# One pool of eight PSUM banks for a fused attention and gated-unit kernel, with the scores of each head in a bank of their own

## The chip, the cores and the metric

The kernel runs on one core of a Trainium2 chip. The metric is the device time of one execution in microseconds (us); the time of a kernel is the median of its runs. Engines are named as the profile names them: PE is TensorE (PEld its weight loads), DVE is VectorE, ACT is ScalarE, POOL is GpSimd, SP is SyncE, which issues the DMAs.

## What is computed

Causal attention with a decay for 8 batches, 8 heads, 576 tokens and 64 features a head, then a gated linear unit with a causal convolution over 5 tokens on the 512 concatenated features (all in fp32 at the borders):

```python
scores = q @ k.T / 8                          # per batch and head, 576 x 576
cum    = cumsum(max(s, 0))
scores = where(causal, -1e9, scores + min(-(cum_i - cum_j), 0))
x      = softmax(scores) @ v                  # heads side by side: 576 x 512 per batch
gate   = sigmoid(sum_k conv_w[k] * x shifted by 4 - k tokens)
out    = (gate * (x @ w_val)) @ w_out
```

## The kernel before

The work is cut into 32 units. Unit n is batch b = n // 4 and head pair p = n % 4, with the head of the pair written hh = 0 or 1. Each unit goes through the same chain, and each link is one task with a name in the code:

- qk_T(b, p) transposes queries and keys of the pair on PE into a PSUM bank, qk_evac copies them out on ACT. tail_T and tail_evac do the same for the last 64 tokens.
- scores(n, step), step 0 to 2, on PE: the causal blocks of the 576 x 576 scores in three steps of 512 columns for each head. Two heads share the 128 rows of PE, so these matmuls use 64 rows each; the planner calls that mode "R" and everything else on PE mode "N". scores4(b, ...) does the last 64 tokens of all four pairs.
- exps(n, step) on ACT: the exponential of one step, from PSUM to the tile P. exp4 is the one for scores4.
- av(n, hh) on PE: 15 matmuls, attention times V', where V' (vprime, on POOL) is V with the decay weights and a column that gives the row sum.
- norm(n) on DVE: two reciprocals (L600) and two multiplications (L602) into xn.
- x_T(n) on PE transposes xn into a bank; x_evac(n) on DVE (L615) copies it to xT.
- tap(n, 0) to tap(n, 4): the five terms of the convolution into gp (L624 on ACT for tap 0 of odd units, else L626 and L628 on DVE). They read the bank of x_T, which is free only after tap 4. tanh(n) on ACT makes the gate.
- val(n, hf) on PE, two halves of the tokens: x @ w_val, for which all four x_evac of the batch must be done. glu(n, hf) on DVE (L659) multiplies with the gate.
- outp(b, i) on PE, out_evac on ACT, store on SP: the second product, five blocks of tokens a batch.

PSUM has eight banks here: four of a kind "m" for everything but scores, and two of a kind "s", each of which is two banks wide and holds one step of scores for both heads:

```python
plan = Plan(dict(m=4, s=2, P=3, gp=2, th=6, ot=3, qkf=3))
ps = slot[tok] = psum.tile([128, 2, 512], FP32, name=f"s{slot['s', tok]}")
nc.scalar.activation(out=slot["Pt", n][:, :, step * 512:(step + 1) * 512], in_=slot["s", n, step], func=AF.Exp, scale=0.125)
```

No loop sets the order of the instructions. Every task is given to a planner (class Plan) with its engine, an estimated duration, a due time (its place in units plus an offset of the table DUE), the tasks that it depends on and the buffers that it takes and gives back. Plan.run plays the tasks through once on the host, in each engine taking the ready task with the earliest due time, and the program is written out in that order. On the chip each engine works its own list strictly in order and waits by semaphore for what it needs. So the durations in the planner set the order, and the chip sets the times. On PE the planner has a rule of its own for going from mode N to mode R and back.

Loads go through SP in the planner's order: queries and keys of a batch (1 MB each, into three buffers "qkf", which POOL casts to bf16), the tails, V, and once the weights w_val (wv), w_out (wo) and conv_w (cw), the last transposed by conv_T on PE and copied to cwT on DVE (L478). Every tap reads cwT.

## Time and profile before

| | |
|---|---|
| time, median of 3 runs | 239.57 us (238.95 to 239.82) |
| time of the profiled execution | 239.43 us |
| its span, first to last instruction | 237.6 us |
| DVE busy | 193.1 us (81%) |
| PE busy | 190.1 us (80%) |
| ACT busy | 184.9 us (78%) |
| POOL busy | 73.5 us (31%) |
| first tap on DVE | 30.98 us |
| last glu on DVE ends | about 225.4 us |

The time lies 1.83 us above the span. Busy time counts an engine's instructions once where they overlap: on ACT and DVE the next instruction starts before the one ahead of it has ended, so the distance from start to start is shorter than the duration that a row gives. A wait in square brackets is time in which the engine stood idle just ahead of that instruction, with the instruction that ended the wait.

### The profile page before, as it was taken

The page shows a single profiled execution, that of the slowest core. Times are in us where ns is not written, and L with a number is a line of the kernel's source. Part 1 is how long each engine was busy: PE and PEld are TensorE (multiplying, and loading weights), DVE is VectorE, ACT ScalarE, POOL GpSimd, SP SyncE. Part 2 cuts the span into 40 slices and gives each one's busy share as a digit, 9 for nine tenths or more (in the row PEclk, how much of TensorE's full clock was granted, in tenths as well). Part 3 has the DMA queues.
Part 4 walks back from the last instruction along what each step waited for, and adds up shares of the span by engine and source line. Part 5 has one row for each costly group of instructions (what it writes and reads, how often), then busy time and mean ns, then how long its engine had stood idle before and what let it go on. Part 6 is the DMA issues. An engine that isn't in the chain of part 4 may idle for free. (4 is left out here: it accounts for less than half of the span.)

```text
span 237.6 us, 6221 instructions
## 1 busy us (share of the span) xinstructions
PE 190.1 (80%) x2561; PEld 124.4 (52%) x2561; DVE 193.1 (81%) x390; ACT 184.9 (78%) x241; POOL 73.5 (31%) x73
## 2 busy tenths in 40 slices
PE   0868746897898999769778797999899998878870
PEld 0546543565656756546546455656666655545420
DVE  4435599999999796998784996999999999999800
ACT  3588878986999999665987678997998998934340
POOL 8400434653953391004910158053035000000000
PEclk9999998899999999988999999999999999999997
DMA  5999789999989987995781402942681120123252
GB/s 153 266 277 375 179 192 320 287 193 243 353 197 263 280 230 229 265 185 179 226 176 29 132 3 87 192 81 88 157 158 44 47 91 22 47 88 110 107 189 75
DMA packets 69230, 40.49 MB, mean 170 GB/s; under 512 B 47109, under 2 KB 63493, under 8 KB 69194
## 3 DMA queue, kind: packets, MB, share of 16 engines
q1 hardware_dynamic: 69194, 40.01, 62.2%
q8 instruction: 22, 0.36, 0.6%
q14 instruction: 14, 0.11, 0.2%
HBM read 30.57 MB, written 9.44 MB: 168 GB/s over the span
## 5 line engine op out<-in xcount | busy, mean ns | idle before, releaser
L628 DVE SCALAR_TENSOR_TENSOR gp<-m,cwT,gp 128x572 f32<-128x572 bf16 (+3 forms) x128 | 103.7, 812 | 5.1 <-ACT gp L624 2.8
L583 ACT ACTIVATE P<-s 128x1024 bf16<-128x1024 f32 x96 | 94.8, 1039 | 11.9 <-PE s L580 8.4
L538 PE MATMUL s<-QKT 64*128 64x128 bf16 (+4 forms) x576 | 40.6, 247 | 10.0 <-ACT P L583 7.4
L500 POOL TENSOR_TENSOR Vp<-vst,w 128x650 bf16<-128x650 f32 x28 | 35.1, 1282 | 40.2 <-DMA vst<-in_v_dram 20.6
L653 PE MATMUL m<-xT,wv 128*128 128x288 bf16 x256 | 40.5, 293 | 7.7 <-DVE glu L659 5.5
L593 PE MATMUL m<-Vp,P 128*128 128x65 bf16 x960 | 39.3, 197 | 4.4 <-DVE gp L628 1.2
L665 PE MATMUL m<-wo,glu 128*128 128x512 bf16 x160 | 40.2, 380 | 2.2 <-DVE gp L628 1.0
L593 PEld LDWEIGHTS <-P 128*128 128x128 bf16 x960 | 35.0, 100 | 12.6 <-issue 3.6
L538 PEld LDWEIGHTS <-QKT 64*128 64x128 bf16 x576 | 20.6, 96 | 27.6 <-issue 18.9
L533 ACT COPY QKT<-m 128x1024 bf16<-128x1024 bf16 x32 | 32.2, 1031 | 3.5 <-PE m L529 3.4
L653 PEld LDWEIGHTS <-wv 128*128 128x128 bf16 x256 | 24.1, 99 | 20.6 <-issue 12.7
L670 ACT COPY ot<-m 128x512 f32<-128x512 f32 (+1 forms) x40 | 23.9, 598 | 14.0 <-PE m L665 11.7
L659 DVE SCALAR_TENSOR_TENSOR glu<-th,m 128x288 bf16<-128x288 f32 x64 | 27.8, 448 | 5.1 <-PE m L653 4.8
L602 DVE TENSOR_TENSOR xn<-m,recs 128x320 bf16<-128x320 f32 x64 | 28.1, 481 | 0.0
L633 ACT ACTIVATE th<-gp 128x576 f32<-128x576 f32 x32 | 22.4, 701 | 6.7 <-DVE gp L628 6.6
L665 PEld LDWEIGHTS <-glu 128*128 128x128 bf16 x160 | 14.2, 98 | 15.5 <-issue 3.6
L529 PE MATMUL m<-ident,qb 128*128 128x128 bf16 x128 | 13.1, 228 | 11.3 <-DVE chalf L432 6.1
L490 POOL CAST qb<-qkf 128x2048 bf16<-128x2048 f32 x7 | 13.2, 1891 | 25.1 <-DMA qkf<-in_q_dram 17.7
L600 DVE RECIPROCAL recs<-m 128x5 f32<-128x5 f32 x64 | 9.2, 176 | 11.0 <-PE m L593 11.0
L529 PEld LDWEIGHTS <-qb 128*128 128x128 bf16 x128 | 8.7, 101 | 16.6 <-issue 7.7
L611 PE MATMUL m<-ident,xn 128*128 128x128 bf16 x160 | 14.3, 220 | 3.6 <-DVE xn L602 2.7
L615 DVE COPY xT<-m 128x576 bf16<-128x576 bf16 x32 | 14.5, 452 | 2.8 <-PE m L611 2.6
(58 smaller groups left out, 151.1 us busy)
## 6 DMA issues: line engine op xcount, KB each, us to landing
out_dram<-ot SPq DMA_DIRECT2D x32, 256.0 KB, 2.1
qkf<-in_q_dram SPq DMA_DIRECT2D x7, 1024.0 KB, 8.6
qkf<-in_k_dram SPq DMA_DIRECT2D x7, 1024.0 KB, 8.8
vst<-in_v_dram SPq DMA_DIRECT2D x28, 256.0 KB, 5.2
vst<-in_v_dram SPq DMA_DIRECT2D x15, 128.0 KB, 4.1
first<-in_q_dram SPq DMA_DIRECT2D x4, 256.0 KB, 3.6
first<-in_k_dram SPq DMA_DIRECT2D x4, 256.0 KB, 3.7
tail<-in_q_dram SPq DMA_DIRECT2D x8, 128.0 KB, 7.7
```

The costliest lines, as they stand in the source:

```text
L500: eng.tensor_tensor(Vps[b % 2][:, :, h], vst[:, :, h], w[:, :, b * 8 + 2 * p:b * 8 + 2 * p + 2].unsqueeze(3).to_broadcast([128, NKB, 2, 65 ...
L533: nc.scalar.copy(QKTs[b % 2][:, :, p, 0:512].rearrange("d w (x j) -> d w x j", j=4), slot["qt", b, p].rearrange("d w (j x) -> d w x j", j=4))
L538: nc.tensor.matmul(ps[:, hh, c0:c0 + nq], QKTs[b % 2][r, 1, p, k0:k0 + 128], QKTs[b % 2][r, 0, p, q0:q0 + nq], **kw)
L583: nc.scalar.activation(out=slot["Pt", n][:, :, step * 512:(step + 1) * 512], in_=slot["s", n, step], func=AF.Exp, scale=0.125)
L593: nc.tensor.matmul(ps[:, qb * 65:qb * 65 + 65], lhsT, Vps[b % 2][:, kb, 2 * p + hh, :], start=(kb == 0), stop=(kb == qb))
L602: nc.vector.tensor_tensor(xns[b % 2][:, :, p * 128 + hh * 64:p * 128 + hh * 64 + 64], pvs[hh][:, :, 0:64], recs[:, n, hh].unsqueeze(2).to_ ...
L628: nc.vector.scalar_tensor_tensor(gp[:, sh:S], x[:, 0:S - sh], cwT[:, c, 4 - sh:5 - sh], gp[:, sh:S], ALU.mult, ALU.add)
L633: nc.scalar.activation(out=th, in_=slot["g", n], func=AF.Tanh, scale=0.5)
L653: nc.tensor.matmul(ps, wv[:, dc, c * 128:(c + 1) * 128], xTs[b % 2][:, dc, 4 + o:4 + o + 288], start=(dc == 0), stop=(dc == 3))
L659: nc.vector.scalar_tensor_tensor(glus[b % 2][:, c, o], slot["t", n][:, o], 1.0, slot["v", n, hf], ALU.add, ALU.mult)
L665: nc.tensor.matmul(ps, glus[b % 2][:, c, WIN[i]:WIN[i] + 128], wo[:, c, :], start=(c == 0), stop=(c == 3))
L670: nc.scalar.copy(ot[r, :], slot["o", b, i][r, :])
```

## The change

Four things change, and the arithmetic does not.

The pool: all eight banks are of one kind, and a step of scores takes two of them, one for each head. Each head's exponential is its own instruction of 512 columns and gives its bank back by itself; so 96 exponentials of 1024 columns become 192 of 512, and the 11 of exp4 become 22.

The planner's choice: of all tasks that are ready on an engine the one with the lowest due time goes first; on PE a task of the other mode has 0.28 (into R) or 13.36 (into N) added to its due time. The old rule on modes is gone.

The table DUE has new numbers, and some durations too (a tap 0.67 to 0.73, norm 1.1 to 1.02).

Some dependencies are put on an earlier task: qk_T and tail_T now wait in the plan for the old scores that qk_evac and tail_evac waited for, x_T for the old val, scores4 and av for what their readers waited for.

```diff
-DUE = dict(av=0.17, norm=-1.06, xt=0.72, xe=0.23, tap=1.91, dtap=0.12, ...
+DUE = dict(av=1.08, norm=-15.2, xt=1.96, xe=-1.95, tap=2.26, dtap=0.21, ...
+STAY = (0.28, 13.36)
...
-                for t in todo[e]:
-                    at = ready_at(t)
...
+                for t in ready[e]:
+                    at = can(t)
...
+                    key = t["key"] + (STAY[t["mode"] == "N"] if e == "PE" and t["mode"] != mode else 0)
+                    if pick is None or (key, t["n"]) < pick[:2]:
+                        pick = (key, t["n"], t)
...
-    plan = Plan(dict(m=4, s=2, P=3, gp=2, th=6, ot=3, qkf=3))
+    plan = Plan(dict(m=8, P=3, gp=2, th=6, ot=3, qkf=3))
...
-        nc.tensor.matmul(ps[:, hh, c0:c0 + nq], QKTs[b % 2][r, 1, p, k0:k0 + 128],
+        nc.tensor.matmul(ps[hh][:, c0:c0 + nq], QKTs[b % 2][r, 1, p, k0:k0 + 128],
...
-        ps = slot[tok] = psum.tile([128, 2, 512], FP32, name=f"s{slot['s', tok]}")
+        slot[tok] = [bank(tok + (hh,), [128, 512]) for hh in range(2)]
...
-    def exps(n, step):
-        nc.scalar.activation(out=slot["Pt", n][:, :, step * 512:(step + 1) * 512], in_=slot["s", n, step],
+    def exps(n, step, hh):
+        nc.scalar.activation(out=slot["Pt", n][:, hh, step * 512:(step + 1) * 512], in_=slot["s", n, step][hh],
...
-                take = [("s", ("s", n, i))] + ([("P", n)] if i == 0 else [])
+                take = [("m", ("s", n, i, hh)) for hh in range(2)] + ([("P", n)] if i == 0 else [])
...
-                es.append(add("ACT", 0.905, n + 0.3 * i, lambda n=n, i=i: exps(n, i), [t],
-                              give=[("s", ("s", n, i))]))
+                es += [add("ACT", 0.48, n + 0.3 * i + 0.01 * hh, lambda n=n, i=i, hh=hh: exps(n, i, hh), [t],
+                           give=[("m", ("s", n, i, hh))]) for hh in range(2)]
```

Since the planner's choice and numbers change, the order on every engine changes. Three places:

On DVE at the start, from the normalisation of unit 1 to the first tap (recs and xn are norm's, wv the cast of w_val, xT the x_evac). Before:

```order
L602 TENSOR_TENSOR xn_116<-m_402,recs 128x5x64
L455 TENSOR_SCALAR wv<-qkf_169 128x2048
L615 COPY xT_118<-m_440 128x576
L600 RECIPROCAL recs<-m_471 128x5
L600 RECIPROCAL recs<-m_487 128x5
```

After, with unit 2's normalisation now ahead of wv and unit 3's behind it, and then cwT and the taps:

```order
L585 TENSOR_TENSOR xn_116<-m_508,recs 128x5x64
L438 TENSOR_SCALAR wv<-qkf_175 128x2048
L583 RECIPROCAL recs<-m_548 128x5
L583 RECIPROCAL recs<-m_612 128x5
L585 TENSOR_TENSOR xn_116<-m_548,recs 128x5x64
L585 TENSOR_TENSOR xn_116<-m_612,recs 128x5x64
L461 COPY cwT<-m_629 128x20
L609 TENSOR_SCALAR gp_388<-m_387,cwT 128x576
```

The cast of w_val moved from behind unit 1 to between units 2 and 3. On SP the load of w_val moved too: from ahead of batch 1's queries, keys and tail to behind them, and that of conv_w stays behind it.

On PE at the same time, behind the last matmul of av(3, 0) (m_515 before, m_548 after). Before, av(3, 1) follows at once:

```order
L593 MATMUL m_515<-Vp_114,P_449 128x65
L593 LDWEIGHTS P_100
L593 MATMUL m_515<-Vp_114,P_100 128x65
L593 LDWEIGHTS P_449
L593 MATMUL m_533<-Vp_114,P_449 128x65
```

After, the transposes of batch 1 (four qk_T and a tail_T) follow, and av(3, 1) and conv_T come behind them:

```order
L576 MATMUL m_548<-Vp_114,P_458 128x65
L576 LDWEIGHTS P_100
L576 MATMUL m_548<-Vp_114,P_100 128x65
L512 LDWEIGHTS qb_105
L512 MATMUL m_566<-ident,qb_105 128x128
```

What moved here are 36 transposes, ahead of the second half of unit 3's attention, on which norm(3), cwT and every tap wait.

On DVE at x_evac of unit 11, the last of batch 2 (glu_120 with th_1439 or th_1593 is the first glu of that batch). Before:

```order
L615 COPY xT_118<-m_1647 128x576
L659 SCALAR_TENSOR_TENSOR glu_120<-th_1439,m_1683 128x288
L659 SCALAR_TENSOR_TENSOR glu_120<-th_1439,m_1691 128x288
L628 SCALAR_TENSOR_TENSOR gp_1648<-m_1647,cwT,gp_1648 128x572
L659 SCALAR_TENSOR_TENSOR glu_120<-th_1596,m_1698 128x288
```

After:

```order
L598 COPY xT_118<-m_1688 128x576
L611 SCALAR_TENSOR_TENSOR gp_1607<-m_1606,cwT,gp_1607 128x574
L611 SCALAR_TENSOR_TENSOR gp_1607<-m_1606,cwT,gp_1607 128x575
L642 SCALAR_TENSOR_TENSOR glu_120<-th_1593,m_1722 128x288
L642 SCALAR_TENSOR_TENSOR glu_120<-th_1593,m_1729 128x288
L642 SCALAR_TENSOR_TENSOR glu_120<-th_1658,m_1735 128x288
L611 SCALAR_TENSOR_TENSOR gp_1689<-m_1688,cwT,gp_1689 128x572
```

Two taps of unit 10 now stand between the copy and the glu, which needs val, which needs the copy.

## Rows read from the trace of the kernel before

**Rows 1.** The page, part 1: busy us, share of span, instructions.

```profile
PE 190.1 (80%) x2561; PEld 124.4 (52%) x2561; DVE 193.1 (81%) x390; ACT 184.9 (78%) x241; POOL 73.5 (31%) x73
```

**Rows 2.** Windows: length, PE, PEld, DVE, ACT, POOL busy, clock, DMA, GB/s.

```profile
31.00:61.00 30.00, 22.40 (x335) 15.63 (x331) 29.47 (x52) 25.50 (x32) 14.82 (x13) 0.94 0.96 255
61.00:151.00 90.00, 76.39 (x1081) 51.13 (x1077) 76.55 (x156) 75.81 (x98) 36.74 (x27) 0.98 0.69 184
151.00:226.00 75.00, 67.81 (x861) 42.63 (x861) 71.97 (x148) 59.73 (x81) 10.00 (x8) 1.00 0.36 95
226.00:237.60 11.60, 4.30 (x21) 1.67 (x19) 0.14 (x1) 3.35 (x6) 0.00 (x0) 0.88 0.38 124
```

**Rows 3.** Waits of DVE, 31 to 226 us: total us, times, longest.

```profile
DVE glu L659 <- PE m L653: 4.8, 6, 1.2
DVE recs L600 <- PE m L593: 3.5, 6, 1.0
DVE gp L628 <- ACT gp L624: 2.8, 5, 1.7
DVE xT L615 <- PE m L611: 2.6, 5, 0.8
```

**Rows 4.** Timeline of DVE: start, us, instruction, [idle before <-releaser].

```profile
92.72 0.45 DVE L659 SCALAR_TENSOR_TENSOR glu<-th,m 128x288 bf16<-128x288 f32 x1 [1.24 <-PE m L653]
...
119.07 1.67 DVE L628 SCALAR_TENSOR_TENSOR gp<-m,cwT,gp 128x572 f32<-128x572 bf16 x2 [1.72 <-ACT gp L624]
...
129.31 0.46 DVE L615 COPY xT<-m 128x576 bf16<-128x576 bf16 x1 [0.55 <-PE m L611]
```

**Rows 5.** Timeline of DVE, two taps of one unit, then a glu.

```profile
121.01 1.66 DVE L628 SCALAR_TENSOR_TENSOR gp<-m,cwT,gp 128x574 f32<-128x574 bf16 x2
122.59 0.45 DVE L659 SCALAR_TENSOR_TENSOR glu<-th,m 128x288 bf16<-128x288 f32 x1
```

**Rows 6.** Timeline of DVE at the start.

```profile
24.06 1.22 DVE L455 TENSOR_SCALAR wv<-qkf 128x2048 bf16<-128x2048 f32 x1
...
29.23 0.19 DVE L600 RECIPROCAL recs<-m 128x5 f32<-128x5 f32 x1 [0.99 <-PE m L593]
...
30.98 0.82 DVE L626 TENSOR_SCALAR gp<-m,cwT 128x576 f32<-128x576 bf16 x1
```

**Rows 7.** Timeline of POOL, the casts of batch 1's queries and keys.

```profile
25.50 1.89 POOL L490 CAST qb<-qkf 128x2048 bf16<-128x2048 f32 x1 [16.90 <-DMA qkf<-in_q_dram]
28.80 1.89 POOL L490 CAST kb<-qkf 128x2048 bf16<-128x2048 f32 x1 [1.41 <-DMA qkf<-in_k_dram]
```

**Rows 8.** Timeline of PE, the last av of unit 3.

```profile
28.68 0.97 PE L593 MATMUL m<-Vp,P 128*128 128x65 bf16 x26 [0.50 <-ACT P L583]
```

**Rows 9.** Groups by line: busy us, mean ns | idle before, releaser.

```profile
L583 ACT ACTIVATE P<-s 128x1024 bf16<-128x1024 f32 x96 | 94.8, 1039 | 11.9 <-PE s L580 8.4
L533 ACT COPY QKT<-m 128x1024 bf16<-128x1024 bf16 x32 | 32.2, 1031 | 3.5 <-PE m L529 3.4
```

**Rows 10.** Timeline of ACT, exponentials of 512 and 1024 columns in a run.

```profile
63.49 0.60 ACT L670 COPY ot<-m 128x512 f32<-128x512 f32 x1
63.95 0.64 ACT L558 ACTIVATE P<-s 128x512 bf16<-128x512 f32 x1
64.44 1.07 ACT L583 ACTIVATE P<-s 128x1024 bf16<-128x1024 f32 x1
65.34 0.64 ACT L521 COPY QKT<-m 128x512 bf16<-128x512 bf16 x1
```

**Rows 11.** Windows in which ACT is fullest; columns as in rows 2.

```profile
60.00:80.00 20.00, 18.03 (x269) 12.15 (x269) 18.64 (x41) 19.49 (x26) 10.41 (x7) 1.00 0.99 257
140.00:160.00 20.00, 17.38 (x238) 11.27 (x238) 17.61 (x36) 19.24 (x26) 10.45 (x9) 1.00 0.48 107
180.00:200.00 20.00, 19.60 (x283) 12.29 (x281) 19.19 (x40) 19.29 (x26) 1.17 (x1) 1.00 0.17 61
```

**Rows 12.** Waits of PE, 31 to 222 us: total us, times, longest.

```profile
PE s L538 <- ACT P L583: 5.5, 12, 1.3
```

More of the change, by code (lines that the diff above doesn't have):

```diff
@@ L220 @@
 NEG = -30000.0
[L224 to L226 removed]
+DUE = dict(av=1.08, norm=-15.2, xt=1.96, xe=-1.95, tap=2.26, dtap=0.21, tanh=3.88, cpe=-1.58, val=4.62,
+           dval=0.97, out=12.49, dout=0.2, oute=12.42, qt=-3.05, qe=4.97, tt=-2, te=-24.47, s4=0.17,
+           vp=-16.42, cast=4.1, lqk=-10.33, lv=-7.3)
+STAY = (0.28, 13.36)
 ON_PE = ()
@@ L252, in run, with can @@
     def run(self):
+        engs = ["SP", "POOL", "PE", "ACT", "DVE"]
         free = {k: [(0.0, i) for i in range(n)] for k, n in self.bufs.items()}
[L254 to L278 removed]
+        idle_at = dict.fromkeys(engs, 0.0)
+        ready = {e: [] for e in engs}
+        after = [[] for _ in self.tasks]
+        for t in self.tasks:
+            t["at"] = 0.0
+            names = {d["n"] for d in t["deps"]}
+            t["left"] = len(names)
+            for i in names:
+                after[i].append(t)
+            if not names:
+                ready[t["eng"]].append(t)
+        mode, dma_free, now = "N", 0.0, 0.0
+        self.order = []
+        def can(t):
+            at = t["at"]
+            for kind in {kind for kind, _ in t["take"]}:
+                c = sum(other == kind for other, _ in t["take"])
+                if len(free[kind]) < c:
+                    return None
+                at = max(at, sorted(free[kind])[c - 1][0])
+            return at
+        while len(self.order) < len(self.tasks):
+            started, later = False, []
             for e in engs:
                 if idle_at[e] > now + 1e-9:
[L281 removed]
+                    later.append(idle_at[e])
                     continue
                 pick = None
[L284 to L289 removed]
+                for t in ready[e]:
+                    at = can(t)
                     if at is None:
@@ L323, in run @@
                 for kind, tok in t["take"]:
-                    slot = min(free[kind])
-                    free[kind].remove(slot)
-                    self.slot[kind, tok] = slot[1]
+                    got = min(free[kind])
+                    free[kind].remove(got)
+                    self.slot[kind, tok] = got[1]
+                t["start"] = now
                 if e == "SP":
@@ L334, in run @@
                     free[kind].append((t["done"] + self.LAG, self.slot[kind, tok]))
-                todo[e].remove(t)
-                t["start"] = start
-                order.append(t)
-                left -= 1
+                ready[e].remove(t)
+                self.order.append(t)
+                later.append(idle_at[e])
                 started = True
-                nxt.append(idle_at[e])
-            if started:
-                continue
-            nxt = [x for x in nxt if x > now + 1e-9]
-            assert nxt, [(e, [(t["key"], t["emit"]) for t in todo[e][:3]]) for e in engs]
-            now = min(nxt)
-        self.order = order
-        return max(t["done"] for t in order)
+                for o in after[t["n"]]:
+                    o["at"] = max(o["at"], t["done"] + (self.LAG if o["eng"] != e else 0.0))
+                    o["left"] -= 1
+                    if o["left"] == 0:
+                        ready[o["eng"]].append(o)
+            if not started:
+                assert later
+                now = min(later)
+        return max(t["done"] for t in self.order)
 def main_path(ctx, tc, q, k, v, s, moe_w_val, moe_conv_w, moe_w_out, out, okcnt):
@@ L563, in scores @@
         b, p = divmod(n, 4)
-        ps = score_bank(("s", n, step))
+        ps = score_banks(("s", n, step))
         if step == 0:
@@ L752, in main_path @@
             on_pe = PE_CONV(b, p)
-            t = T["xt", n] = add("PE", 0.3, n + DUE["xt"], lambda n=n: x_T(n), ns,
-                                 take=[("m", ("x", n))] + ([] if on_pe else [("gp", n)]), mode="N")
+            t = T["xt", n] = add("PE", 0.3, n + DUE["xt"], lambda n=n: x_T(n),
+                                 ns + [T.get(("val", n0 - 8 + c, hf)) for c in range(4) for hf in range(2)],
+                                 take=[("m", ("x", n))] + ([] if on_pe else [("gp", n)]))
             T["xe", n] = add("DVE", 0.37, n + DUE["xe"], lambda n=n: x_evac(n),
```

114 lines of the change are left out of this document (33 added, 81 removed).

## The prediction

> **What bounds the kernel now.** I read the busy shares first. DVE, PE and ACT lie within 3% of each other, each near 80% [rows 1], so the totals name no bound. The windows do: from the first tap at about 31 us to the last glu at about 226 us DVE is busy 29.47 of 30, 76.55 of 90 and 71.97 of 75 us, together 178.0 of 195 [rows 2]. PE reaches 166.6 and ACT 161.0 in the same 195 us. So DVE sets the pace in the first and the last of the three windows, and in the middle one, where all three engines are busy some 85% of 90 us, they wait for each other in turn. Ahead of 31 us DVE has nothing to do but wait for the first units, and the last 11.6 us are the last output blocks and their stores, with DVE nearly idle [rows 2]; the order of that tail is almost the same in the changed kernel, so I leave it as it is.
>
> The span is therefore: the time of the first tap, plus DVE's work, plus DVE's waits, plus the tail. The waits are 4.8 + 3.5 + 2.8 + 2.6 = 13.7 us in 22 pieces [rows 3]; the 3.3 us that are missing to 17.0 are gaps too short for that view. DVE executes the same instructions after the change, so what can move is the first tap, the waits, and how tightly the taps follow each other.
>
> **The change, part by part.** The sum is made on the span of 237.6 us.
>
> *The waits of DVE: -6.7 us.* Most of them are round trips: DVE hands something to PE or ACT and then has too little other work until it comes back. Three kinds show in the rows. A glu straight behind the last x_evac of its batch stood 1.24 us, the time of val on PE; a tap 1 behind its own x_evac waited 1.72 us for tap 0 on ACT; an x_evac straight behind its norm waited 0.55 us for x_T [rows 4]. In the order of the instructions I counted the places where less than about 1 us of other DVE work stands in such a round trip (for the third kind, none or one short instruction), from unit 2 on. Before there are 12: 2, 7 and 3 of the three kinds. After there are 5: two glu (batches 3 and 5; the first is also a tap 1 place), two more tap 1 (units 19 and 29), and one x_evac (unit 20). The place of batch 2, worth 1.24 us and 0.51 behind it, has got two taps as cover. A second count says the same: behind a norm there stand on average 4.2 taps of older units still to do, 2.4 before, so DVE has a longer list to live from when PE is late. By the first count 5/12 of 13.7 us, that is 5.7, would be left; but 3.5 us of the waits are those of norm for av, which are no such places. I take half, 7.0 us left. Bounds: all left (0) to the five places at the cheapest price, 5 x 0.55 = 2.7 left (-11.0).
>
> Why should the new order keep its places on the chip? PE waited 12 times, 5.5 us in all, to write scores into one of only two double banks [rows 12], and val or av standing behind such a wait came late. With eight single banks scores can also go where a transpose or a val has just left, and each bank is free after half the exponential. The number of banks is the same, though: what scores get, av, x_T and val must do without. That is why I do not take the low end.
>
> *Taps in a row: -1.4 us.* Two successive taps of one unit start 0.85 us apart (two take 1.66 us, each 0.81), and a tap is followed by another kind of instruction after 0.73 us (121.01 + 0.85 + 0.73 = 122.59) [rows 5]. The order before has 64 pairs of neighbouring taps of one unit, the order after 52: 12 x 0.12 = 1.4 us, where DVE is full. Bounds -1.4 to 0.
>
> *The first tap: +1.0 us.* Every tap needs cwT. Before, wv ran at 24.06 in a pause of DVE, norm(3) began at 29.23 and the first tap at 30.98 [rows 6]. Now w_val is loaded behind batch 1's queries, keys and tail. Batch 1's two loads had landed at about 25.5 and 28.8 [rows 7], 3.3 us apart, as the second and third megabyte; now w_val is the third, with the tail's quarter of a megabyte ahead of it, so 28.8 + 0.8 = 29.6 us, estimated from that spacing. Then wv 1.2 us, and from norm(3) to the first tap the 1.75 us of before, less the half of norm's pause that PE no longer makes: about 32.0 to 32.5, and I take 1.0 us later. On PE, av(3, 1) and conv_T now stand behind four qk_T and a tail_T, and the last av cannot be done much before 29.65 (28.68 + 0.97) [rows 8], since it waits for the last exponentials; if av(3, 1) must also wait for an evacuation of 1.03 us [rows 9] to get its bank, norm(3) starts up to 2 us later than before. Bounds 0 to +2.5. In return batch 1's keys land one load earlier, which gives PE and ACT a lead; DVE is full until 61 us [rows 2], so that earns nothing at once.
>
> *Twice as many exponentials: +1.0 us.* From start to start an exponential of 1024 columns takes 65.34 - 64.44 = 0.90 us and one of 512 columns 64.44 - 63.95 = 0.49 us; a copy of 512 columns takes 0.46 [rows 10]. A pair so costs 0.02 to 0.08 us more than the whole, 96 pairs [rows 9] 2 to 7.7 us of ACT, and I take 0.08, the row of the same operation. ACT has the room over the whole (78% busy [rows 1]) but not in three stretches of 20 us where it is busy 19.2 to 19.5 us [rows 11]. The 96 exponentials lie over some 200 us, so about 10 in such a stretch: 0.8 to 1.0 us more against 0.5 us of room in the first and 0.8 in the others, some 0.3 to 0.5 over. I charge two of the three at 0.5, 1.0, since in the middle one DVE has 2.4 us of room of its own. Bounds 0 to +3.0 (all of the 1.0, three times).
>
> *A rule that speaks against this part.* The Trainium skill ("ScalarE: Activation LUTs", section "What ACT_TABLE_LOAD costs") gives an activation a fixed 186 ns beside 0.833 ns a column, of which some 93 ns overlap the next one; by that a pair costs 93 ns more than the whole, 9 us in all, and the three stretches 1.5 to 2 us in place of 1.0. For 1024 columns it gives 1039 ns, which is the mean in rows 9. The Trainium skill ("Perfetto Trace Analysis", section "Optimizing Scalar/DVE Operations") says that larger operations pay where an engine is saturated, and that breaking them up pays where it is not but makes bubbles on others.
>
> *Switches of PE between the modes* go from 130 to 112 in the order. PE is not the bound between 31 and 61 us or behind 151 us [rows 2], and no row prices a switch by itself; nothing is charged. The DMAs move, but behind the start no wait of DVE in rows 3 ends with one; nothing is charged there either.
>
> Sum: 237.6 - 6.7 - 1.4 + 1.0 + 1.0 = 231.5 us. The profiled execution took 1.83 us over its span and lay 0.14 us under the median, so 231.5 + 1.83 + 0.14 = 233.5 us.
>
> **The rivals.**
>
> *Full cover* (chance 0.20). The places are all that is left: -11.0 for the waits, the taps -1.4, the first tap +1.0, ACT's stretches at 0, since a full ACT would itself make waits: 226.2 of span, 228.2 us. For it: DVE shows that it can run at 98% for 30 us and at 96% for 75 us [rows 2]. Against it: in the middle 90 us PE and ACT are as full as DVE.
>
> *The waits only move* (0.13). The change does not do what it says: eight banks are handed out before and after, and a step of scores still needs two at once. DVE then waits for av and val as long as before, at other places: 237.6 - 1.4 + 1.0 + 1.0 = 238.2, 240.2 us. For it: the waits of norm and glu, 8.3 of the 13.7 us, are for PE, and PE works strictly in order.
>
> *ACT becomes the bound* (0.06). The waits shrink as forecast, but the split lands on the path in full: 7.7 in place of 1.0 us, 238.2 of span, 240.2 us. For it speak the three full stretches [rows 11]; against it 161.0 of 195 us [rows 2]. The Trainium skill's sentence on saturated engines ("Perfetto Trace Analysis", "Optimizing Scalar/DVE Operations") is for this case.
>
> *av waits for its exponentials* (0.12), the slower case. The order gives av less cover: between the last score step of a unit and its av stand 6.0 PE tasks on average, 10.0 before, and the scores are 1.5 steps ahead of av, 2.5 before. A PE task is 190.1 us / 350 tasks = 0.54 us, so the cover is some 3.3 us, of which the two last exponentials take 1.0. It decides where ACT is more than 2.3 us behind PE. Then PE stands at av, makes no scores, and ACT runs dry in turn. The price of a unit is the wait of norm for av where it has no cover, 0.99 us at the start [rows 6]. If that strikes six units, those of the three full stretches at two each, beside waits that stay: 237.6 - 1.4 + 1.0 + 1.0 + 5.9 = 244.1, 246.1 us.
>
> **How the numbers follow.** The forecast has 0.47, full cover 0.20, moved waits 0.13, ACT bound 0.06, av waiting 0.12, and 0.02 is for what I do not see. A difference under 0.5%, 1.2 us, cannot be told from no change here. The forecast and full cover are faster but for 0.01 of the forecast's late end: 0.66. Moved waits and ACT bound lie within 0.5% (238.4 to 240.8) for the most part: 0.18. Slower keeps 0.16. The range goes from 227.5 us, a little under full cover since the first tap may not move (-1.0), to 240.7 us, over the two cases in the middle; it leaves out av waiting, what I do not see and some of the ends.
>
> **What would show it.** The waits of DVE between the first tap and the last glu: near 7 us if I am right, under 4 for full cover, 13 or more if they only moved. The first tap at about 32 us. Exponentials of 512 columns 0.46 to 0.52 us apart in a run; ACT busy at 187 to 193 us. If av waits, PE's waits for exponentials at L576 grow from nearly nothing to several us and DVE's waits ahead of norm beyond 3.5 us. The forecast is wrong if the first tap comes behind 34 us, if one stretch shows ACT full with DVE waiting for it, or if the tail behind the last glu is not 11.6 us or so.

## The result and the profile after

The changed kernel takes **227.4 us** (median of 4 runs, 225.5 to 229.9) beside 239.7 us for the kernel before (239.0 to 241.2): a ratio of 0.945, with a 95% interval of 0.935 to 0.955. (Ratios here leave out a run that lies over 1.5% above the fastest of its kernel, so this one is that of three runs, while medians and ranges are of all.) The forecast was 233.5 us, the low end of its range 227.5. The sign was right, and the gain, 12.3 us, is twice the 6.1 forecast. Run three times more beside other kernels the changed one gave medians of 227.6, 227.4 and 228.8 us.

The profiled execution was the longest of its four, 229.9 us with a span of 228.0. Its busy shares answer to [rows 1]:

```profile
PE 194.5 (85%) x2561; PEld 129.0 (57%) x2561; DVE 190.3 (83%) x390; ACT 189.0 (83%) x348; POOL 73.4 (32%) x73
```

The windows answer to [rows 2]; the last glu now ends at 215.8 us, so the third one is ten us shorter. The columns are the length, PE, PEld, DVE, ACT and POOL busy, the clock granted to PE, and the DMAs' share and GB/s:

```profile
31.00:61.00 30.00, 24.34 (x293) 16.67 (x291) 29.35 (x55) 22.35 (x42) 13.79 (x12) 0.78 1.02 251
61.00:151.00 90.00, 84.31 (x1207) 56.45 (x1205) 84.88 (x176) 85.64 (x156) 37.17 (x27) 0.98 0.71 190
151.00:216.00 65.00, 60.26 (x771) 38.14 (x769) 63.52 (x132) 55.89 (x104) 10.00 (x8) 0.99 0.38 108
216.00:228.00 12.00, 5.27 (x19) 1.98 (x17) 0.00 (x0) 2.92 (x5) 0.00 (x0) 0.78 0.30 106
```

The middle window holds the gain. Of its 90 us PE was busy 76.4, DVE 76.6 and ACT 75.8 [rows 2]; now they are busy 84.3, 84.9 and 85.6. All three filled up together, by 8 to 10 us each: what was taken away is the time in which they waited for each other in turn. The tail behind the last glu is 12.2 us in both kernels.

DVE's waits from 31 to 216 us answer to [rows 3]; the first row lies ahead of the first tap:

```profile
DVE wv L438 <- DMA qkf<-in_moe_w_val_dram: 3.6, 1, 3.6
DVE xT L598 <- PE m L594: 1.6, 2, 1.2
DVE recs L583 <- PE m L576: 1.5, 3, 1.0
DVE glu L642 <- PE m L636: 1.4, 2, 1.0
```

Behind the first tap 4.5 us in 7 pieces are left of 13.7 us in 22. Waits for ACT are gone (2.8 before), glu's fell from 4.8 to 1.4, norm's from 3.5 to 1.5. The profiles of the three later sets of runs of the same kernel show 4.5, 3.0 and 2.4 us.

PE's waits, which answer to [rows 12]. L521 is scores, L576 is av. Scores need nothing from norm (xn) but its bank:

```profile
PE m L521 <- DVE xn L585: 2.7, 3, 1.5
...
PE m L521 <- ACT P L566: 1.0, 3, 0.7
...
PE m L576 <- ACT P L566: 0.2, 1, 0.2
```

The waits of scores for exponentials fell from 5.5 us in 12 to 1.0 in 3, and av, which the slower rival had waiting, waits once for 0.2 us. But scores now wait for banks that DVE gives back: 2.7 us for norm's, and by two more rows 0.8 for glu's and 0.4 for the taps'. With 1.3 us for qk_evac and tail_evac, all rows of scores make 6.2 us, no less than before. What fell are PE's other waits for a bank, above all those of val, whose largest row before was

```profile
PE m L653 <- DVE glu L659: 5.5, 8, 1.3
```

and is now 0.6 us. From 31 us to some 3 us ahead of the last glu all rows of that view add up to 25.6 us before and 11.4 after (9.9 to 11.9 in the three later profiles of this kernel).

The start on DVE, which answers to [rows 6]:

```profile
31.26 1.23 DVE L438 TENSOR_SCALAR wv<-qkf 128x2048 bf16<-128x2048 f32 x1 [3.57 <-DMA qkf<-in_moe_w_val_dram]
...
33.63 0.82 DVE L609 TENSOR_SCALAR gp<-m,cwT 128x576 f32<-128x576 bf16 x1
```

The first tap starts at 33.63 us, 2.65 later than before: w_val landed at 31.3 us, not at the 29.6 estimated. In the three later profiles of this kernel it landed at 31.9, 30.0 and 29.9 us, and the first tap started at 34.3, 32.3 and 32.5.

### The profile page after: what moved, and what is told of

Its sections match the earlier page's. It is cut to its first block, busy times and chain, and to the rows that moved or that the text cites. A ratio compares the mean times of both kernels' runs of the same rounds, so it can differ in the third digit from the quotient of the medians.

```text
span 228.0 us, 6320 instructions
## 1 busy us (share of the span) xinstructions
PE 194.5 (85%) x2561; PEld 129.0 (57%) x2561; DVE 190.3 (83%) x390; ACT 189.0 (83%) x348; POOL 73.4 (32%) x73
## 4 chain that ended last, share of the span: by engine, by line
DVE 69%; PE 12%; SPq 8%; DMA 6%; issue 2%; ACT 1%; ACTq 0%
DVE gp L611 38%; DVE xn L585 10%; DVE glu L642 8%; DVE gp L609 5%; DMA qkf<-in_moe_w_val_dram 4%; DVE xT L598 4%; PE m L636 3%; PE m L648 3%; SPq L470 3%; SPq L478 2%; DVE recs L583 2%; SPq L489 2%; PE m L512 2%; PE m L576 1%; DMA out_dram<-ot 1%
## 5 line engine op out<-in xcount | busy, mean ns | idle before, releaser
L566 ACT ACTIVATE P<-m 128x512 bf16<-128x512 f32 x192 | 104.4, 672 | 11.0 <-PE m L563 9.1
L521 PE MATMUL m<-QKT 64*128 64x128 bf16 (+4 forms) x576 | 45.8, 253 | 9.5 <-DVE xn L585 2.9
L648 PE MATMUL m<-wo,glu 128*128 128x512 bf16 x160 | 41.9, 397 | 1.0 <-DVE gp L611 0.3
L521 PEld LDWEIGHTS <-QKT 64*128 64x128 bf16 x576 | 21.7, 98 | 31.4 <-issue 18.8
L576 PE MATMUL m<-Vp,P 128*128 128x65 bf16 x960 | 37.6, 197 | 1.8 <-ACT P L566 1.4
L576 PEld LDWEIGHTS <-P 128*128 128x128 bf16 x960 | 35.1, 100 | 5.6 <-ACT P L566 1.6
L516 ACT COPY QKT<-m 128x1024 bf16<-128x1024 bf16 x32 | 33.4, 1069 | 5.6 <-PE m L512 5.4
L653 ACT COPY ot<-m 128x512 f32<-128x512 f32 (+1 forms) x40 | 25.1, 651 | 9.4 <-PE m L648 6.7
L642 DVE SCALAR_TENSOR_TENSOR glu<-th,m 128x288 bf16<-128x288 f32 x64 | 27.6, 445 | 1.4 <-PE m L636 1.4
L616 ACT ACTIVATE th<-gp 128x576 f32<-128x576 f32 x32 | 24.5, 767 | 1.6 <-DVE gp L611 1.6
L648 PEld LDWEIGHTS <-glu 128*128 128x128 bf16 x160 | 15.1, 101 | 18.1 <-issue 6.3
L512 PEld LDWEIGHTS <-qb 128*128 128x128 bf16 x128 | 9.7, 107 | 11.7 <-DVE chalf L415 6.1
L473 POOL CAST kb<-qkf 128x2048 bf16<-128x2048 f32 x7 | 13.3, 1894 | 4.4 <-DMA qkf<-in_k_dram 4.4
```

Source lines behind the costliest of these rows:

```text
L473: eng(qkbs[which][b % 2].rearrange("p j (h d) -> p h j d", h=8)[:, hs], f.rearrange("p h (j d) -> p h j d", j=4))
L512: nc.tensor.transpose(pt[:, which, j * 128:(j + 1) * 128], qkbs[which][b % 2][:, j, p * 128:(p + 1) * 128], ident)
L516: nc.scalar.copy(QKTs[b % 2][:, :, p, 0:512].rearrange("d w (x j) -> d w x j", j=4), slot["qt", b, p].rearrange("d w (j x) -> d w x j", j=4))
L521: nc.tensor.matmul(ps[hh][:, c0:c0 + nq], QKTs[b % 2][r, 1, p, k0:k0 + 128], QKTs[b % 2][r, 0, p, q0:q0 + nq], **kw)
L566: nc.scalar.activation(out=slot["Pt", n][:, hh, step * 512:(step + 1) * 512], in_=slot["s", n, step][hh], func=AF.Exp, scale=0.125)
L576: nc.tensor.matmul(ps[:, qb * 65:qb * 65 + 65], lhsT, Vps[b % 2][:, kb, 2 * p + hh, :], start=(kb == 0), stop=(kb == qb))
```

## The experiments

**Order and banks apart.** The change does two things at once: another order, and another way to share the banks. The first run is the changed kernel, unchanged; the two others have the order of before.

> The changed kernel again, for the spread of its times and for a profile at a higher granted clock. Its four first runs took 225.49 to 229.89 us, the lower the granted clock (0.959 to 0.927) the longer. Expected by both theories: 225 to 230 us, and the time falling by about 1.4 us for each 0.01 of mean granted clock, if the clock is what spreads the runs.

Measured: 227.6 us (225.7 to 229.8). A straight line through these four runs falls by 1.2 us for each 0.01 of mean clock, one through all 18 runs of this kernel by 1.0. That they go together does not show which makes which.

The second has the order of before with the cut exponentials, and hands the eight banks out of one pool along that order:

```diff
-        ps = slot[tok] = psum.tile([128, 2, 512], FP32, name=f"s{slot['s', tok]}")
+        slot[tok] = [psum.tile([128, 512], FP32, name=f"m{slot['s', tok][hh]}") for hh in range(2)]
...
+                got = sorted(free)[:2 if kind == "s" else 1]
```

> The kernel before, with its order of tasks kept on every engine, but the scores of each head in a bank of their own with their own exponential, and all eight banks handed out in turn along that order (the bank that has been free longest first). Theory 1, the order: the gain of the change is that the new order gives DVE other work in the round trips; then this kernel gains nothing beyond PE's 5.5 us of waits for exponentials, most of which are not on DVE's path, and ACT has 96 x 0.05 = 5 us more: 238 to 241 us, DVE's waits from the first tap on near 13 us. Theory 2, the banks: scores no longer wait for one of two double banks and val and av behind them come in time; then most of the late waits of DVE (some 5 of the 7.8 us that are not round trips) go here too: 232 to 235 us.

Measured: 237.3 us, ratio 0.989 [0.985, 0.993]. DVE's waits from 31 to 226 us:

```profile
DVE gp L630 <- ACT gp L626: 4.8, 8, 1.8
DVE glu L661 <- PE m L655: 4.2, 5, 1.6
DVE recs L602 <- PE m L595: 2.6, 7, 0.9
DVE xT L617 <- PE m L613: 2.1, 5, 0.6
```

That is 13.7 us again, the sum of [rows 3] to the tenth, in other shares: the waits are as theory 1 has them, and the time lies 0.7 us under its range and 2.3 above that of theory 2. The third has the order of before, its fixed banks, and only the exponentials are cut in two:

```diff
-        nc.scalar.activation(out=slot["Pt", n][:, :, step * 512:(step + 1) * 512], in_=slot["s", n, step],
-                             func=AF.Exp, scale=0.125)
+        for hh in range(2):
+            nc.scalar.activation(out=slot["Pt", n][:, hh, step * 512:(step + 1) * 512], in_=slot["s", n, step][hh],
+                                 func=AF.Exp, scale=0.125)
```

> The kernel before, its order and its fixed banks kept (two pairs of banks for scores), with each step's exponential cut into two instructions of 512 columns. It measures the split alone: ACT 4 to 8 us busier by the rows (0.05 to 0.08 us a pair). Theory 1 (order): 239 to 242 us. Theory 2 (banks): the first bank of a pair is free 0.48 us earlier but is taken only together with the second, so it says 239 to 242 us too; what it tells apart is the price of the split from the worth of the pool in the run with the pool.

Measured: 242.1 us, ratio 1.008 [1.006, 1.011], with 16.4 us of DVE's waits up to the last glu. So cutting the exponentials costs 2.3 us by itself, the pool more than gives it back under the same order (237.3 from 242.1), and the other ten of the 12 us come only with the new order.

**Does the new order need the pool?** Two runs, from either side. In the first the changed kernel keeps its planner, and each task's due time is its place in the changed kernel's own schedule, but four banks serve scores alone and four the rest:

```diff
+    starts = {t["n"]: t["start"] for t in plan.order}
+    def apart(toks):
+        return tuple(("s", tok) if kind == "m" and tok[0] in ("s", "s4") else (kind, tok) for kind, tok in toks)
+    for t in plan.tasks:
+        t.update(done=None, key=starts[t["n"]], take=apart(t["take"]), give=apart(t["give"]))
+    plan.bufs = dict(plan.bufs, m=4, s=4)
+    plan.total = plan.run()
```

> The changed kernel, its cut exponentials and its planner, with four banks for scores and four for everything else in place of one pool of eight. The planner is given, as the due time of each task, the time at which that task stands in the changed kernel's own schedule, so that the order differs from it only where a bank of the right kind is not free. Theory A (the order can only be kept because any bank may serve anything): PE must put off av, val, x_T or scores until a bank of the right kind is free, DVE's waits come back, and the time is 235 us or more. Theory B (the order is the gain and the pool only a way of writing it down, since eight banks are eight banks): DVE's waits grow by under 3 us, and the time is under 230.5 us.

Measured: 254.7 us, ratio 1.056 [1.049, 1.063], 27 us above the changed kernel beside it. DVE's waits behind its first tap (which starts at 40.5 us), and PE's largest:

```profile
DVE glu L643 <- PE m L637: 6.0, 10, 1.5
DVE xT L599 <- PE m L595: 5.2, 9, 1.6
DVE gp L612 <- ACT gp L608: 4.7, 7, 1.2
DVE recs L584 <- PE m L577: 3.3, 8, 0.8
```

```profile
PE s L522 <- ACT P L567: 5.1, 14, 1.4
```

19.9 us of DVE's waits, with a row of 0.7 that is left out, and PE's wait for a bank for scores is back at what it was in [rows 12]. Part of the 27 us is the start, since the first tap comes 7 to 8 us later. In this way the order could not be had with the banks apart. But another may be, which is the second run: the changed kernel's planner, the old banks and whole exponentials, and due times that a short search on the planner found for them.

```diff
-DUE = dict(av=1.08, norm=-15.2, xt=1.96, xe=-1.95, tap=2.26, dtap=0.21, tanh=3.88, cpe=-1.58, val=4.62, ...
+DUE = dict(av=0.156, norm=-4.212, xt=1.125, xe=-78.869, tap=2.144, dtap=0.238, tanh=3.046, cpe=101.903, ...
...
-    plan = Plan(dict(m=8, P=3, gp=2, th=6, ot=3, qkf=3))
+    plan = Plan(dict(m=4, s=2, P=3, gp=2, th=6, ot=3, qkf=3))
```

> The other side: the changed kernel's planner with the old banks (four single ones, two double ones for scores) and whole exponentials, with due times of its own that a search of some minutes on the planner found for these banks; the changed kernel's own due times don't suit them. Theory A (without the pool no order gives DVE its cover): DVE's waits from the first tap on stay at 9 us or more, and the time is 233 to 240 us. Theory B (a better order is to be had without the pool): DVE's waits fall under 6 us, and the time under 230 us. A result between these would say that both have a share. The search was short, so a long time speaks less than a short one.

Measured: 235.4 us, ratio 0.980 [0.976, 0.984]. The time is that of theory A, the waits lie between the two theories. DVE's waits behind the first tap:

```profile
DVE glu L642 <- PE m L636: 3.1, 5, 1.4
DVE gp L611 <- ACT gp L607: 1.9, 4, 0.9
DVE recs L583 <- PE m L576: 1.4, 5, 0.3
DVE xT L598 <- PE m L594: 0.9, 2, 0.5
```

7.3 us, half of before; and PE still waits 5.0 us in 14 pieces for a bank for scores. Some 5 of the 13 us are to be had by order alone, and in all that was tried the other 8 came only with the pool and the cut exponentials that go with it. How much more a long search would find for the old banks stays open.

**The places.** The forecast counted the places on DVE where an answer is needed at once, 12 before and 5 after, and priced them. Two runs change only DVE's list (and, in the first, which bank serves which task). In the first, the order of before (with pool and cut exponentials, 237.3 us) has its norms and x_evacs moved one or two instructions earlier, so that about 4 such places are left:

```diff
+    for n in (7, 9, 11, 15, 19, 21, 23, 25, 27):
+        ahead(T["norm", n], 2)
+        ahead(T["xe", n], 2)
+    for n in (6, 16, 19):
+        ahead(T["norm", n], 1)
```

> The order of before with the shared banks and the cut exponentials (237.3 us, 13.7 us of DVE's waits from 31 us to 226 us), and of its order only DVE's queue is changed: norms and x_evacs of units 7 to 27 stand one or two instructions earlier, so that of the 12 places where DVE gives out a result and needs the engines' answer at once about 4 are left. PE's and ACT's queues stay as they are, and so does the work. Theory 1 (the order makes DVE's waits, by these places): the waits fall by 5 to 6 us, to about 8, and the time to 231 to 233 us. Rival (the places are only where a lag shows that PE and ACT have anyway): the waits turn up at other instructions, their sum stays at 12 or more, and the time at 236 us or more.

Measured: 251.7 us, ratio 1.045 [1.038, 1.053], 14 us *slower* than without the mending. The rival's bounds hold (12 us or more, 236 us or more), but it had no such loss. DVE's waits from 31 us to the last glu, and unit 19's norm and x_evac on DVE:

```profile
DVE recs L655 <- PE m L648: 11.3, 12, 2.1
DVE xT L670 <- PE m L666: 9.3, 10, 2.3
DVE glu L714 <- PE m L708: 4.2, 4, 1.9
DVE gp L683 <- ACT gp L679: 4.1, 4, 2.3
```

```profile
148.88 0.19 DVE L655 RECIPROCAL recs<-m 128x5 f32<-128x5 f32 x1 [1.84 <-PE m L648]
...
155.46 0.46 DVE L670 COPY xT<-m 128x576 bf16<-128x576 bf16 x1 [2.29 <-PE m L666]
```

Without the mending that norm waited 0.2 us and that x_evac 0.55 us. The waits doubled to 28.9 us and changed their name: DVE now asks for av and x_T before PE, whose list is the old one, comes to them. While it stands there the taps behind it are late, and ACT waits for them in turn (15.8 us ahead of th between 31 and 216 us, 6.6 without the mending).

The second run goes the other way. The changed kernel, with PE's and ACT's lists as they are, gets 11 of the old tight places back on DVE:

```diff
+    for n in (6, 16, 19):
+        behind(T["xe", n], T["norm", n], 0)
+    for n, gap in ((9, 1), (11, 1), (15, 0), (19, 1), (21, 1), (23, 1), (25, 1)):
+        if seq.index(T["tap", n, 1]) > seq.index(T["xe", n]) + 1 + gap:
+            behind(T["tap", n, 1], T["xe", n], gap)
+    behind(T["glu", 8, 0], T["xe", 11], 0)
+    behind(T["glu", 8, 1], T["glu", 8, 0], 0)
```

> The changed kernel (227.5 us, 4.5 us of DVE's waits behind the first tap) with its banks, its cut exponentials and PE's and ACT's queues, and in DVE's queue 11 of the old tight places put back (two glus, seven first taps on DVE, two x_evacs stand again right behind the instruction whose answer they need). Theory 1: the waits come back with the places, by their mean of about 0.5 us each: 4 to 7 us, to 231 to 234 us. Rival: the cover is that of PE's and ACT's queues, which still run ahead; DVE's waits grow by under 1.5 us, and the time stays under 229 us.

Measured: 240.0 us, ratio 1.000 [0.995, 1.004]. All of the gain is gone. DVE's waits behind the first tap:

```profile
DVE gp L664 <- ACT gp L660: 5.6, 7, 1.5
DVE glu L695 <- PE m L689: 3.9, 6, 1.6
DVE xT L651 <- PE m L647: 3.6, 4, 1.8
DVE recs L636 <- PE m L629: 2.0, 4, 0.8
```

15.1 us: 10.6 more for 11 places, about 1 us each, twice what the expectation took. Theory 1 holds in its direction and was too cheap; the rival, that PE and ACT run ahead far enough by themselves, is out.

**The start.** The load of conv_w, the last half of unit 3's av and conv_T stand earlier, and wv's scaling is on POOL, where it takes 5.4 us in place of 1.2; the banks are dealt out anew along this order:

```diff
+    put(T0["cwl"], T["ld", 1, 0])
+    put(T["avh", 3, 1], T["qt", 1, 0])
+    put(T0["cwt"], T["qt", 1, 0])
...
+        on = nc.gpsimd if nm in ("wv",) else nc.vector
```

> The changed kernel with its order from the fifth batch on untouched; in the start the load of conv_w stands ahead of the second batch's q on SP, the second half of the fourth unit's product with V and the transposition of conv_w stand ahead of the second batch's first transposition on PE, and the scaling of w_val (1.25 us on DVE) is on POOL. If DVE's queue bounds the time from its first tap on (theory 1), the first tap moves from about 34.0 us to about 31.5 us and the whole end with it: 225 us, 2 to 2.5 us less than the changed kernel. Rival (what DVE gains in the start it waits for later, since PE or ACT are late there): under 1 us of it reaches the end.

Measured: 228.9 us, ratio 0.952 [0.946, 0.959], no gain. DVE in this run, from the first tap to norm of unit 7, the last of the second batch:

```profile
29.91 0.82 DVE L629 TENSOR_SCALAR gp<-m,cwT 128x576 f32<-128x576 bf16 x1
...
35.73 3.37 DVE L631 SCALAR_TENSOR_TENSOR gp<-m,cwT,gp 128x572 f32<-128x572 bf16 x4 [1.60 <-ACT gp L627]
40.53 0.46 DVE L618 COPY xT<-m 128x576 bf16<-128x576 bf16 x1 [1.43 <-PE m L614]
...
62.40 0.19 DVE L603 RECIPROCAL recs<-m 128x5 f32<-128x5 f32 x1 [0.97 <-PE m L596]
```

And the same norm in the changed kernel:

```profile
62.38 0.19 DVE L583 RECIPROCAL recs<-m 128x5 f32<-128x5 f32 x1 [1.00 <-PE m L576]
```

The first tap came 3.7 us earlier, 3.6 us of that went into waits by 43 us (1.6 for ACT, 2.0 for x_T), and unit 7's norm starts at the same time with the same wait. ACT is busy 10.00 of the 10 us from 34 to 44 us here, and 13.00 of the 13 from 31 to 44 in the changed kernel: its list is as long there as DVE's. So an earlier first tap gains nothing, and the rival held. By the rows a later one does cost: in the changed kernel's profile DVE has no wait from the first tap to 61.4 us, and the chain that ended last runs through w_val's load, as the table at the end of this section shows too.

**The clock ahead of 62 us.** In the changed kernel's profile two stretches ahead of 62 us are nearly wholly at the lower of the clock's two levels (1.2 and 2.4 GHz); ahead of each PE was busy 4.1 of 6 us and 2.4 of 4 us:

```profile
31.00:37.00 6.00, 4.08 (x65) 2.80 (x63) 5.59 (x10) 6.00 (x12) 0.88 (x1) 1.00 1.00 201
37.00:44.00 7.00, 6.26 (x51) 3.29 (x51) 6.83 (x10) 7.00 (x15) 5.00 (x4) 0.54 1.11 325
...
50.00:54.00 4.00, 2.37 (x47) 1.68 (x45) 4.00 (x12) 0.70 (x2) 2.45 (x2) 1.00 0.84 177
54.00:62.00 8.00, 7.57 (x66) 5.77 (x66) 7.34 (x13) 6.50 (x11) 4.01 (x4) 0.57 0.98 287
```

Some small matmuls and transposes (84 in all, 128 columns, the identity with itself; "90" in the expectations) stand in PE's waits in the first 53 us:

```diff
+    WARM = {("s", 0, 1): 4, ("s", 0, 2): 4, ("s", 1, 0): 12, ("s", 1, 1): 4, ("qt", 0, 2): 8, ("s", 2, 0): 4, ...
+    def warm(o, key):
+        for _ in range(WARM.get(key, 0)):
+            nc.tensor.matmul(o, ident, ident, start=True, stop=True)
```

> The changed kernel with some 90 small extra matmuls and transpositions on PE, all in its first 53 us and in tiles that are overwritten or started anew behind them, put where PE waits; the outcome is as before. In the profiled runs of the changed kernel PE has the lower granted clock in three stretches before 62 us. If these stretches make the time (the changed kernel's own runs spread over 4 us, the shortest with the highest mean clock), they become fewer, the mean clock goes to 0.95 or more, the runs lie nearer together, and the median falls by 1 to 2 us to about 226 us. Rival (the low clock stands in stretches in which DVE has cover, and the spread has another cause): the median stays within 0.7 us of 227.5 us, or rises by the 2 us or so that the extra work lasts.

Measured: 225.4 us (224.2 to 229.2), ratio 0.938 [0.929, 0.946], the profiled one with a mean clock of 0.985 and a span of 222.9. It overlaps with the changed kernel's, so it was run again beside it, with a third kernel that also scales w_out on POOL:

> The changed kernel, beside the two runs below and on the same chip: 224.4 to 229.9 us, as in its runs so far.

> The changed kernel with the 90 small extra matmuls once more, in more rounds, since its first four times (224.2 to 229.2 us, median 225.4) overlap with those of the changed kernel. If the low clock ahead of 62 us makes part of the changed kernel's time, the median lies 1.5 to 2.5 us under that of the run beside it and the mean clock at 0.97 or more. Rival: under 0.7 us apart, the first result was chance.

> As the run before, and the scaling of w_out (1.22 us of DVE, in the stretch from 44.5 to 54.5 us in which DVE is busy 10.0 of 10.0 us) is on POOL. If DVE's queue bounds the time there, 1.0 to 1.2 us less than the run before. Rival (the next unit's av is not there any earlier, and DVE waits for it, as with the earlier start): under 0.4 us less.

Measured: 228.8 us (0.954 [0.949, 0.959] to before), 226.9 us (0.944 [0.939, 0.948]) and 226.4 us (0.944 [0.939, 0.948]). The intervals of the first two just miss each other: the kernel with the extra work on PE is 1.9 us faster, at a mean clock of 0.974 over its runs beside 0.946. Over all sets the medians are 228.3 us (18 runs) and 226.4 (10 runs). That it is faster through the clock fits, but is not shown by itself. Taking 1.22 us from DVE ahead of 62 us (with the banks dealt out anew) gives nothing that can be told from zero. The same stretch behind PE's pause in the last of the three, at the full clock:

```profile
50.00:54.00 4.00, 3.16 (x43) 1.82 (x40) 3.92 (x8) 2.18 (x5) 3.58 (x3) 1.00 1.06 208
54.00:62.00 8.00, 7.10 (x107) 5.32 (x108) 8.00 (x18) 8.00 (x14) 5.59 (x5) 1.00 1.09 312
```

PE does 107 matmuls there, none of them an extra one, 66 in the changed kernel. In the profile of the second of the three the clock of that stretch is 0.79, with 80 matmuls. The two ideas together, with the changed kernel beside them on the same chip:

> The changed kernel once more, beside the three runs below, on the same chip: 225.5 to 229.9 us, DVE's waits behind the first tap 1.8 to 4.5 us. It is there to compare with; both theories expect the same.

> The changed kernel with the earlier start (the load of conv_w and the last product with V of the first batch ahead, the scaling of w_val on POOL), with the scaling of w_out on POOL too (1.22 us less on DVE), and with the 90 small extra matmuls on PE in the first 53 us; the outcome is as before. If the earlier start was lost only because PE was at its low clock behind it (in the run with the start alone DVE waited 1.6 us for ACT and 3.6 us for x_T between 34 and 44 us, with the clock granted at 0.75 there), this keeps some 2 us of it and the 1.2 us: 222 to 223.5 us. Rival (what is gained ahead of 62 us is lost there whatever the clock, since the first av of the second batch comes when it comes): 224.2 to 226 us, as with the extra matmuls alone.

Measured: 227.4 us for the changed kernel (0.940 [0.932, 0.949]) and 227.2 us (0.947 [0.943, 0.951]) for both together: no gain beside it. The earlier start is lost again, with 2.4 us of waits for x_T and 1.0 us for ACT by 43 us. The mean clock of that profile is 0.98, but 0.83 between 34 and 44 us (0.67 in the run with the start alone), so a full clock in that stretch was not tried with the earlier start. (The 3.6 us for x_T in the expectation are those of the whole run; 2.0 of them lie ahead of 44 us.) The rival held, at a time 1 us above its own.

Over the nine profiles of the changed kernel and of these variants the span varies from 222.9 to 228.7 us, and the start of unit 7's norm from 58.9 to 62.9 us; from that norm to the end it is 163.8 to 166.3 us in all nine. In the changed kernel's own four, 224.7 to 228.0 us, 2.5 of the 3.3 us lie ahead of that norm. Most of what varies ahead of it is there at the first tap, which follows the landing of w_val:

| profile | first tap, us | unit 7's norm, us | span, us |
|---|---|---|---|
| changed, of the result | 33.63 | 62.38 | 228.0 |
| changed, beside the old orders | 34.28 | 62.93 | 228.0 |
| changed, beside both together | 32.34 | 60.54 | 225.5 |
| changed, beside the extra matmuls | 32.47 | 60.39 | 224.7 |
| extra matmuls | 31.29 | 58.92 | 222.9 |
| extra matmuls again | 34.03 | 62.01 | 226.5 |

From the first tap to that norm it is 27.6 to 28.8 us in all six, while the first tap moves by 3.0 us. So when w_val lands is a rival of the clock for the spread of the runs, and no run here fixes it; in the last profile the clock is full from the start to 37 us and w_val lands late all the same.

## Why the forecast went wrong

The times of the runs follow DVE's waits behind the first tap, nearly, as the forecast's first part has it:

| kernel | DVE's waits, us | span, us |
|---|---|---|
| changed | 4.5 | 228.0 |
| new planner, old banks | 7.3 | 232.5 |
| order of before, pool | 13.7 | 235.3 |
| before | 13.7 | 237.6 |
| changed, places back | 15.1 | 240.5 |
| order of before, cut exponentials | 16.4 | 241.2 |
| changed order, banks apart (first tap at 40.5) | 19.9 | 253.8 |
| order of before, places mended | 28.9 | 251.4 |

So this part of the forecast holds. Term by term, on the span of the profile:

- *The waits: -6.7 forecast, -9.2 measured* (-10.7 and -11.3 in the two profiles with 3.0 and 2.4 us left). This is the step that failed. The count gave 2.7 us left by the five places alone, and I went up to 7.0 because scores, av, x_T and val share the same number of banks as before, so that what one gets another must do without. The runs show no such trade; it went the other way. Scores wait as long as before (6.2 us, of which 3.9 for banks from DVE), and it is the others that find a bank: PE's waits ahead of val fell from 7.3 to 2.4 us, ahead of av from 3.2 to 0.4, ahead of qk_T from 4.7 to 1.0. Tie four of the eight banks to scores again and the waits are back: 5.0 and 5.1 us of scores for exponentials, 5.3 and 6.4 ahead of val, 4.0 and 7.1 ahead of av. The pool alone does not do it either: under the old order all of PE's waits make 24.9 us with it, 25.6 without. So the number of banks, the same in all these runs, did not set the price; pool and order together did, and what each did for a single wait is not shown. The Trainium skill ("Perfetto Trace Analysis", section "Matmul Optimizations") says to see that all eight banks are used; the kernel before has all eight too, and by the runs here how they are handed out, with the exponentials and the order that go with each way, is worth 8 us between the two kernels with the new planner. Of the five places named, three show in each profile of the changed kernel: the first glu of batch 3 with 1.00 us, that of batch 5 with 0.37, the x_evac of unit 20 with 0.45; the two taps wait for nothing. The rows are these, and the first of them is the longest of the waits that stay whatever the clock:

```profile
116.15 0.45 DVE L642 SCALAR_TENSOR_TENSOR glu<-th,m 128x288 bf16<-128x288 f32 x1 [1.00 <-PE m L636]
...
134.10 0.46 DVE L598 COPY xT<-m 128x576 bf16<-128x576 bf16 x1 [1.20 <-PE m L594]
...
146.76 0.46 DVE L598 COPY xT<-m 128x576 bf16<-128x576 bf16 x1 [0.45 <-PE m L594]
...
163.60 0.94 DVE L642 SCALAR_TENSOR_TENSOR glu<-th,m 128x288 bf16<-128x288 f32 x2 [0.37 <-PE m L636]
```

  The other two large ones, 1.20 us at unit 18 (second row) and 1.00 at unit 7's norm, come with a stretch of low clock: in two of the three later profiles of the same kernel the first is gone, and the second is 0.35 us or nothing.
- *What a place is worth.* The count was right for the wrong reason. Places put back cost 1 us each, not the 0.5 that the rows of before suggest, and mending them on DVE's list alone made 14 us of loss. By these two runs a place is not a fault of DVE's list alone: it is where three lists do not meet, and moving entries of one list moved the meeting points of the others.
- *Taps in a row: -1.4 forecast.* DVE's busy time fell by 2.8 us, 193.1 to 190.3, with the same instructions. The 12 pairs fewer are worth 12 x 0.08 = 1.0 us, from 0.81 to 0.73 [rows 5]. The rest I put down, without a run of its own, to the 15 waits that are gone: an instruction that follows at once starts some 0.1 us ahead of the recorded end of the one before it, one behind a wait does not, so each wait costs that much more than its row says.
- *First tap: +1.0 forecast, +2.65 measured (1.4 to 3.3 over the four profiles of the changed kernel).* The load was estimated 1.7 us too early for this profile, 0.3 for two of the others. In the range seen the end goes with it; an earlier one gains nothing, since ACT's list is as long there.
- *Exponentials: +1.0 forecast, nothing to be seen in DVE's waits.* No run takes the cut out of the changed kernel alone, so a part may stand ahead of 44 us, where ACT is full. Six of them in a row take 3.02 us from the first's start to the last's end:

```profile
165.95 3.02 ACT L566 ACTIVATE P<-m 128x512 bf16<-128x512 f32 x6
```

  With 0.64 us for the last [rows 10] that is (3.02 - 0.64) / 5 = 0.48 us from start to start, so a pair costs 0.05 us more than the whole, not 0.08. (The 1.5 to 2 us that the forecast gives the three stretches at its other price do not follow from it: ten pairs a stretch at 9 / 96 us lie some 0.8 us over the room of all three.) ACT's busy time grew by 4.1 us, within the 187 to 193 that the forecast asked for. DVE hardly ever waits for ACT any more. In the order of before the same cut cost 2.3 us: whether it is paid is a matter of cover, too.

The sum of what was measured, -9.2 - 2.8 + 2.65 = -9.4 us, answers to 237.6 - 228.0 = 9.6 us; it is bookkeeping along DVE and shows no cause. The case that came nearest is the rival "full cover" (228.2 us, chance 0.20): waits near the low bound, ACT's stretches at nothing. That its time is only 0.8 us off is in part luck: its span, 226.2 us, is 1.8 short of the profile's, since it has more off the waits than was measured and less on the first tap, and it is set beside a median 2.5 us under the time of that profiled execution. My argument against it was that PE and ACT are as full as DVE in the middle 90 us. It was the wrong way round: three engines at 85% that wait for each other have 13 us to give, and they gave 8 to 10 (ACT's share is in part its longer exponentials). Beside that, I added the profiled execution's distance to the median as a constant; the changed kernel's runs lie up to 4 us apart, which the runs of before shown ahead of the forecast did not suggest.

## What to carry to other kernels

Where several engines stand at 85% in the same stretch and wait for each other in turn, look at that idle time as a gain that may be had, not as a sign that none is left: here 8 to 10 of 13 us were. Price a tight round trip by the lists of all engines that take part in it, and be wary of mending one engine's list alone: here that cost 14 us, where fitting all lists together, with the pool, won 12. Buffers tied to one use can make waits even when their number is enough; try one pool, and measure it with an order that was made for it: with the old order it was worth 2.4 us here, the price of the cut exponentials already taken off.

## What was not expected of the hardware

PE's granted clock fell to its lower level behind stretches in which PE had pauses (4.1 of 6 us busy, 2.4 of 4 us busy), and the kernel with 84 matmuls of no use in such pauses was 1.9 us faster than the one beside it. It is not settled which pause sets it off: the lower level comes at somewhat different times in each profile of the same kernel, and in the second set of runs with the extra matmuls the clock was 0.70 between 37 and 44 us in spite of them. Nor is it settled how much of the 1.9 us is the clock, since the landing of w_val moved the start by up to 3 us from one profile to the next. The kernel with the extra matmuls stood at 0.938 and 0.944 of the kernel before in its two sets of runs, the changed kernel at 0.940 to 0.954 in its four.
